# Other places for two hundred operations of the first attention block in a kernel whose order is written out by hand

## The chip, the cores and the metric

The kernel runs on one core of a Trainium2 chip. The metric is device time in microseconds (us) for one execution; a figure for a kernel is the median of its runs. The kernel before was run three times: 416.27, 416.80 and 418.25 us, median 416.8 us.

## What is computed

The input is x of 2048 rows by 512 columns in bf16. Four residual layers follow one another: x + A, x + B, x + A, x + B, each on the layer norm of x.

```python
# A: sliding-window attention, 32 heads of 16, window 256
qkv = layernorm(x) @ wqkv
scores = einsum("bhqd,bhkd->bhqk", q, k) * 16**-0.5      # masked to 0 <= q - k < 256
x = x + (softmax(scores) @ v) @ wo
# B: linear attention, phi(t) = where(t > 0, t + 1, exp(t)) + 1e-6
kv, z = einsum("bhsd,bhse->bhde", phi(k), v), phi(k).sum(s)
x = x + (phi(q) @ kv / (phi(q) @ z)) @ wo
```

## The kernel before, in words

The 2048 rows are cut into four groups of 512 (I = 0 to 3), each of four tiles of 128 rows. For each group of the first layer the kernel makes the layer norm (`ln_tile`), transposes it (`transpose`, into `xnT`), and multiplies by the weights (`proj`): queries into `qT`, keys into `kall` (spread over two columns so that two heads can share a matmul), values into `vst`, from where DMAs scatter them into `vbd`.

The attention itself (`scores`, `pv_group`) goes in runs. One run is 8 to 16 small matmuls on TensorE (L823) that write four banks of PSUM: two banks (the first pair) are read by one exponential on ScalarE (L834), two (the second pair) by another (L837). Both write one of seven `pt` buffers. Then the edges of the window are zeroed in `pt` by masks: on VectorE as a multiplication with a 0/1 tile (`tri`, L852), on GpSimd as `affine_select` (L857), one instruction for each 128x256 piece. When all masks of a set of runs are done, `pv_group` multiplies `pt` by `vbd` on TensorE (L880), and VectorE divides by the sums (L893, L894). The TensorE results of `proj` are taken out of PSUM by VectorE or ScalarE (`evac`, L527, `k_spread`, L786 and L788).

PSUM has eight banks. `psb` is all eight of them, and each operation that takes a bank is told which one. A bank is written again only when its last reader is done, and the wait for that is put in by the framework.

The order of everything is written out in the string `ORDER`. Each word is one operation: its number, the engine that issues it (P TensorE, A ScalarE, V VectorE, G GpSimd, S the SP queue that issues DMAs, H a transfer that has landed, no instruction), and the places that it takes, one digit for each ring. `163P42` is operation 163 on TensorE, a run of scores whose first pair is banks 4 and 5 and whose second pair is banks 2 and 3. `675P5` is the first half of a projection (two matmuls of 512 columns) in bank 5; its second half, `676P`, and the reader of the bank, `677V`, follow. A word such as `2F4` is a fill: two matmuls of the identity into bank 4 whose result nobody reads (L463). Each engine executes its own words strictly in the order in which they stand; how the words of different engines are interleaved has no effect but through the waits for data and for places.

Operations named below: scores 163, 188, 204, 210, 235, 240, 395, 416, 432, 437, 469, 474 with the two exponentials whose numbers follow each (163: 164 and 165; 432: 433 and 434); projections 100/101, 102/103, 358 to 360 (an evacuation, 360, on VectorE), 355 to 357 (keys, 357 on VectorE), 650 to 653 (keys; 653 is the spreading of half of them), 678 to 680 (values), 675 to 677 (queries); masks 213, 409, 420, 421; 422, the first of the `pv_group` operations of group I = 1; 647, the reciprocal root of a layer norm (`rstd`, which takes two instructions on GpSimd, L595 and L596, or two on ScalarE, L592 and L593); 648, 649 and 664, the normalisation that uses it, the DMA transpose of it, and the projection that reads it.

Of the kernel before, what the change touches and what calls it, by code (L numbers as in the profile page):

```python
# [234 lines left out]
494V 495G 493V 507A 693S 943V1 2F4 496P5 179V 501P4 508A 497P 511P06 498P 512A 510V 509G 502P 180V1 499P 47S 503P 513A
500V 504P 181G 516P02 686P5 517A 514V 505V 940S 184V3 518A 3F7 521P06 671P4 45S 48H 687P 522A 519V 947V2 672P 688V 523A
527P20 674V 948S 265P5 266P 529A 524V 526G 661P7 673V 944S 515G 662P 528A 267V 525G 261P6 520V 694P40 663A 689S 531V
532G 262P 695A 530V 533P7 263V 534P 696A 535P 272V0 699P42 538P6 700A 539P 698G 540P 182G01 536P 701A 541P 537V 704P04
273G 705A 542V 952P3 543S1 703G 953P 268V2 706A 709P06 668P2 547S0 954V 669P 710A 274V3 970P3 670V 555S2 711A 715P04
708V 971P 702V 697V 716A 973P7 714G 551S3 972V 974P 707G 712V 717A 731P20 975V 949P6 732A 713V 950P 719G 720V 43S 718V  # L240
733A 951V 2F7 736P42 721P7 722P 738A 723P 734G 726P6 724P 737A 727P 725V 728P 729P 741P24 740G 730V 552P7 739G 743A 553P
977P6 742A 554V 746P40 978P 748A 544P7 979V 545P 747A 744V 752P20 980S 745V 958P6 575V 754A 959P 750G 546V 735G 749V
269G 753A 2F5 768P40 960V 185G 751V 769A 755V 2F7 773P62 756V 757V 8V 774A 186G2 763P5 758P4 764P 567V0 775A 759P 187S
765P 559V1 760P 770A 766P 776G 761P 777G 275S 767V 778P26 270G1 955P0 779A 762V 956P 556P1 780A 957V 976S 783P42 557P
# [1204 lines left out]
```

## Time and profile before

| | |
|---|---|
| runs | 416.27, 416.80, 418.25 us; median 416.8 |
| span of the profiled execution, first to last instruction | 414.3 us |
| TensorE busy | 395.2 us (95%) |
| ScalarE busy | 368.8 us (89%) |
| VectorE busy | 355.0 us (86%) |
| GpSimd busy | 239.2 us (58%) |
| chain that ended last, by engine | PE 66%, ACT 15%, DVE 12%, issue 4%, POOL 2% |

The page gives the span of the profiled execution and no other time of it; the median of the runs is 2.5 us above the span. Times within the trace count from the start of the span. PE is TensorE, ACT ScalarE, DVE VectorE, POOL GpSimd, SPq the SP queue. "L837" is line 837 of the kernel. Where instructions overlap their start and end in an engine's pipeline (two exponentials overlap by a tenth of a microsecond or more), the distance from start to start is what an instruction costs its engine.

### The profile page before, as it was taken

The page shows a single profiled execution, that of the slowest core. Times are in us where ns is not written, and L with a number is a line of the kernel's source. Part 1 is how long each engine was busy: PE and PEld are TensorE (multiplying, and loading weights), DVE is VectorE, ACT ScalarE, POOL GpSimd, SP SyncE. Part 2 cuts the span into 40 slices and gives each one's busy share as a digit, 9 for nine tenths or more (in the row PEclk, how much of TensorE's full clock was granted, in tenths as well). Part 3 has the DMA queues.
Part 4 walks back from the last instruction along what each step waited for, and adds up shares of the span by engine and source line. Part 5 has one row for each costly group of instructions (what it writes and reads, how often), then busy time and mean ns, then how long its engine had stood idle before and what let it go on. Part 6 is the DMA issues. An engine that isn't in the chain of part 4 may idle for free.

```text
span 414.3 us, 15373 instructions
## 1 busy us (share of the span) xinstructions
PE 395.2 (95%) x6277; PEld 219.3 (53%) x6347; DVE 355.0 (86%) x844; ACT 368.8 (89%) x496; POOL 239.2 (58%) x505
## 2 busy tenths in 40 slices
PE   7998999999999999999999999999999999999995
PEld 3565555555555555643565555555555555565342
DVE  5899898888769988689998999998789588889895
ACT  5999999999999999678999999999999999977731
POOL 7578524344576667923774688554427476585432
PEclk9999999999999999999999999999999999999998
DMA  8233226440313122100032212322111311300024
GB/s 245 83 95 100 64 76 110 110 77 24 89 25 80 35 55 26 28 4 0 22 72 41 55 45 64 71 38 53 41 49 34 54 30 40 54 14 14 3 69 138
DMA packets 65306, 24.11 MB, mean 58 GB/s; under 512 B 46160, under 2 KB 65232, under 8 KB 65232
## 3 DMA queue, kind: packets, MB, share of 16 engines
q1 hardware_dynamic: 63168, 21.65, 23.5%
q10 hardware_dynamic: 2064, 1.44, 1.1%
q8 instruction: 50, 0.82, 0.8%
q14 instruction: 24, 0.20, 0.2%
HBM read 6.29 MB, written 2.10 MB: 20 GB/s over the span
## 4 chain that ended last, share of the span: by engine, by line
PE 66%; ACT 15%; DVE 12%; issue 4%; POOL 2%; ACTq 0%; POOLq 0%; DVEq 0%
PE psb L537 41%; PE psb L880 14%; PE psb L823 8%; ACT pt L834 7%; ACT pt L837 7%; DVE pt L852 2%; DVE kall L788 1%; PE psb L995 1%; DVE qT L527 1%; PE psb L566 1%; DVE kall L773 1%; PE psb L463 1%; DVE vst L527 1%; PE psb L1106 1%; DVE ln L661 1%
## 5 line engine op out<-in xcount | busy, mean ns | idle before, releaser
L857 POOL TENSOR_SCALAR_AFFINE_SELECT pt<-pt 128x256 bf16<-128x256 bf16 x285 | 121.3, 453 | 110.2 <-ACT pt L837 66.7
L837 ACT ACTIVATE pt<-psb 128x1024 bf16<-128x1024 f32 (+2 forms) x156 | 156.2, 1017 | 4.4 <-PE psb L823 3.0
L834 ACT ACTIVATE pt<-psb 128x1024 bf16<-128x1024 f32 (+2 forms) x156 | 156.7, 1014 | 3.6 <-PE psb L823 2.3
L880 PEld LDWEIGHTS <-pt 128*128 128x128 bf16 x2880 | 81.4, 96 | 16.5 <-issue 5.0
L880 PE MATMUL psb<-vbd,pt 128*128 128x34 bf16 x2880 | 85.1, 178 | 2.4 <-ACT pt L834 1.0
L537 PE MATMUL psb<-xnT,wA 128*128 128x512 bf16 (+1 forms) x305 | 65.1, 335 | 2.2 <-DVE o_sb L894 0.3
L537 PE MATMUL psb<-wB,xnT 128*128 128x512 bf16 x237 | 62.4, 379 | 1.7 <-issue 0.5
L823 PE MATMUL psb<-qT,kall 32*128 32x256 bf16 (+4 forms) x1664 | 62.6, 242 | 0.6 <-ACT pt L834 0.4
L537 PEld LDWEIGHTS <-xnT 128*128 128x128 bf16 x384 | 33.4, 97 | 37.0 <-issue 5.3
L823 PEld LDWEIGHTS <-kall 32*128 32x128 bf16 x1664 | 28.0, 92 | 45.8 <-issue 42.2
L852 DVE TENSOR_TENSOR pt<-pt,tri 128x512 bf16<-128x512 bf16 (+1 forms) x133 | 49.5, 399 | 2.8 <-ACT pt L837 1.9
L537 PEld LDWEIGHTS <-wA 128*128 128x128 bf16 x320 | 27.4, 97 | 26.1 <-issue 7.7
L537 PE MATMUL psb<-woA,oT 128*128 128x512 bf16 x120 | 32.8, 380 | 1.2 <-issue 0.6
L537 PE MATMUL psb<-wA,xnT 128*128 128x512 bf16 x115 | 32.3, 380 | 1.5 <-ACT pt L837 0.5
L537 PE MATMUL psb<-xnT,wB 128*128 128x512 bf16 x119 | 32.1, 380 | 0.9 <-issue 0.5
L537 PE MATMUL psb<-wkv,pqT 128*128 128x512 bf16 (+1 forms) x126 | 30.2, 373 | 0.5 <-issue 0.2
L894 DVE TENSOR_TENSOR o_sb<-psb,rall 128x256 bf16<-128x256 f32 x64 | 27.2, 424 | 2.4 <-DVE rall L893 0.2
L893 DVE RECIPROCAL rall<-psb 128x16 f32<-128x16 f32 x64 | 16.1, 251 | 13.7 <-PE psb L880 9.4
L661 DVE BATCH_NORM_STATS2 ln<-xres 128x6 f32<-128x512 f32 (+1 forms) x39 | 26.6, 682 | 1.2 <-DMA xres<-in_A_x_dram 1.1
L596 POOL TENSOR_TENSOR ln<-ln,mhalf 128x1 f32<-128x1 f32 x38 | 22.0, 578 | 3.2
L948 ACT ACTIVATE pks<-psb 128x512 bf16<-128x512 f32 x32 | 19.5, 614 | 3.8 <-PE psb L537 3.4
L527 DVE CAST qT<-psb 128x512 bf16<-128x512 f32 (+1 forms) x32 | 19.2, 602 | 3.9 <-PE psb L537 3.7
(133 smaller groups left out, 523.6 us busy)
## 6 DMA issues: line engine op xcount, KB each, us to landing
vbd<-vst SPq DMA_DIRECT2D x128, 34.0 KB, 1.9
wB<-in_B_wqkv_dram SPq DMA_DIRECT2D x6, 256.0 KB, 3.5
out_dram<-ost SPq DMA_DIRECT2D x10, 128.0 KB, 1.8
xres<-in_A_x_dram SPq DMA_DIRECT2D x4, 256.0 KB, 3.2
xnT<-xn SPq DMA_TRANSPOSE x50, 2.4
out_dram<-ost ACTq DMA_DIRECT2D x5, 128.0 KB, 2.8
wA<-in_A_wqkv_dram SPq DMA_DIRECT2D x1, 512.0 KB, 7.5
xres<-in_A_x_dram SPq DMA_DIRECT2D x1, 512.0 KB, 8.7
```

Source lines behind the costliest of these rows:

```text
L527: (nc.scalar.copy if e == "ACT" else nc.vector.tensor_copy)(dst(), src())
L537: nc.tensor.matmul(t["t"][:], lhsT=lhs(c), rhs=rhs(c), start=(c == 0), stop=(c == NCT - 1))
L596: nc.gpsimd.tensor_tensor(out, out, mhalf[:, 0:1], op=ALU.pow)
L661: nc.vector.bn_stats(t["st"], x())
L823: nc.tensor.matmul(psb[:, sT.k + x if x < 2 else sS.k + x - 2, at * 64:(at + w) * 64], lhsT=kbd[half(m)][32 * x:32 * x + 32, tt, m % 4, :, :],
L834: nc.scalar.activation(body[:, 0:2, 0:w_all, :], psb[:, sT.k:sT.k + 2, 0:w_all * 64].rearrange("p x (s c) -> p x s c", c=64), ACT.Exp, sca ...
L837: nc.scalar.activation(body[:, 2:4, 0:w_all, :], psb[:, sS.k:sS.k + 2, 0:w_all * 64].rearrange("p x (s c) -> p x s c", c=64), ACT.Exp, sca ...
L852: nc.vector.tensor_tensor(v, v, mt, op=ALU.mult)
L857: nc.gpsimd.affine_select(out=v, in_=v, compare_op=ALU.is_ge, fill=0.0, base=1 if kind == 0 else -2, pattern=[[0, 4], [2 * sg, 64]], chann ...
L880: nc.tensor.matmul(t["O"][:, x, g, :, :], lhsT=parts[b][0][:, s0:s0 + 2, :], rhs=vbd[half(m)][:, m % 4, :, 4 * tt + g, :], start=(n == 0), ...
L894: nc.vector.tensor_tensor(o_sb[:, u0:u0 + nu, P * tt:P * tt + P].rearrange("p u (h e) -> p u h e", e=DH), Ov[:, :, :, 0:DH], r.to_broadcas ...
L948: nc.scalar.activation(dst(), ps()[:], ACT.Exp)
```

## The change

Only `ORDER` changes. The first words of each engine are the same, and from about 70 us of the trace on each engine has the words that it had, in the order that it had. Between them, from about 20 us on, some two hundred words stand at other places of their engines' orders. Forty-eight operations take other places in rings, most of them banks of PSUM. Twenty-five go to another engine: 11 masks from GpSimd to VectorE (162, 196, 203, 208, 213, 233, 239, 243, 409, 440, 472), 11 masks from VectorE to GpSimd (197, 228, 245, 398, 404, 421, 435, 441, 446, 450, 452), the evacuation 103 from VectorE to ScalarE, the root 647 from GpSimd to ScalarE, and the key spreading 653 from ScalarE to VectorE. On SP some twenty words change places: the scatter 119 goes ahead of 115, the loads 31, 29 and 51 go forward, the load 35 and the scatter 685 go back behind 637 and 681, and the transpose 176 stands beside 172. The number of fills stays, and one of them (3F0) goes to bank 1. The stretch in both orders (the words are wrapped anew from there to the end of the string, which makes the whole diff long):

```diff
-136V 25S 112P0 345V3 151A 149G 113P 152A 159P64 118A 337V31 140G 102P2 114V 161A 35S 128P1 346G 129P 103V 130P 131P 160A
-342V1 163P42 153G 132V 26H 165A 115S 347V2 162G 3F0 188P06 164A 634V1 100P2 189A 166G 141P5 154P4 101V 155P 142P 36H
-143P 190A 635G 144P 28H 352V0 193P02 145V 156P 119S 12G 157P 194A 108P6 158V 167P7 168P 191G 169P 195A 109V 170P 199P04
-171V 348P6 200A 353P3 196G 349V 338P7 172S0 354V 343P6 201A 339V 204P02 638V0 379P7 29S 205A 380P 202G 344V 636V32 192G
-206A 381V 2F5 210P04 361P6 639G 637S 642V1 362P 211A 208G 110P7 363V 212A 31S 203G 224P02 30H 198G 640V0 225A 383P5 213G
-111V 384P 197V 382S 226A 643G 229P06 385V 214P4 215P 230A 646V0 216P 32H 358P5 644V3 231A 647G 217P 228V 235P02 641S
-218V 359P 209G 236A 207G 355P7 360V 219P6 645S 237A 933V2 240P04 356P 241A 648V1 220P 239G 357V 221P 649S 232G 222P 233G
-242A 246P02 227V 387P7 234G 386S 247A 223V 388P 238G 245V 389V 248A 395P04 13G 664P6 396A 665P 249V 934G 390S 250P7 667V
...
-255P6 407A 366V 394S 410P02 256P 398V 257P 411A 404V 409G 258P 678P7 259V 412A 679P 416P04 680V 260S3 417A 657P3 414G
-408V 415G 658P 276V 418A 650P2 264S2 660V 432P06 651P 413V 434A 419G 420V 51S 367P5 421V 368P 433A 659V 422P4 423P 369V
-424P 653A 33S 436G 437P06 425P 438A 652V 427P5 428P 426V 429P 439A 430P 442P02 431V 376P4 443A 440G 377P 942G 34H 370P5
-444A 378V 447P06 371P 441V 935V20 448A 682P4 372V 683P 449A 435V 453P02 684V 675P5 454A 676P 446V 451G 685S 452V 450V
-455A 2F4 469P60 677V 445V 471A 457V 2F4 474P24 458V 456V 49S 937V1 475A 464P1 459P0 465P 476A 460P 466P 41S 461P 470A
...
+150P42 27S 112P0 151A 345V3 113P 149G 152A 25S 28H 118A 159P64 100P1 102P3 128P2 129P 130P 131P 337V22 101V 342V0 114V
+119S 115S 31S 29S 51S 52H 32H 30H 26H 161A 160A 346G 132V 347V3 162V 352V1 163P46 165A 164A 103A 153G 140G 166G 634V3
+3F1 188P06 141P5 142P 143P 144P 154P4 155P 156P 189A 190A 157P 193P02 194A 195A 158V 145V 167P7 168P 169P 108P6 170P
+199P04 109V 171V 353P3 348P2 343P6 338P7 354V 349V 339V 197G 191G 635G 344V 638V2 196V 201A 200A 202G 639G 204P42
+379P7 380P 205A 206A 381V 636V01 642V0 640V2 2F5 210P04 361P6 362P 110P7 211A 176S0 172S1 382S 641S 637S 35S 212A
+224P20 225A 226A 383P5 384P 363V 111V 209G 207G 643G 644V1 213V 198G 192G 229P26 385V 646V1 214P4 215P 216P 217P 230A
+235P02 358P5 359P 231A 647A 203V 208V 218V 233V 360V 648V2 645S 649S 219P6 355P7 237A 236A 356P 933V1 234G 13G 12G
+228G 357V 240P24 220P 221P 222P 242A 241A 246P04 387P7 388P 386S 247A 248A 223V 227V 389V 239V 244G 238G 232G 934G
...
+393V 243V 405P04 364P7 406A 407A 255P6 365P 410P02 256P 941V3 366V 411A 412A 257P 258P 678P7 416P40 679P 657P3 658P
+417A 935V20 945V2 259V 415G 414G 403G 398G 413V 680V 408V 660V 409V 432P64 650P2 651P 418A 419G 421G 420V 394S 260S2
+264S3 49S 367P1 368P 652V 369V 653V 659V 434A 433A 422P0 423P 424P 437P46 425P 427P1 428P 429P 430P 438A 439A 442P42
+426V 431V 376P0 377P 444A 443A 682P1 447P62 683P 370P5 371P 378V 435G 684V 440V 449A 448A 453P02 675P4 676P 445V 372V
+441G 677V 454A 455A 2F4 469P60 2F4 474P24 456V 458V 457V 446G 436G 451G 450G 942G 452G 471A 464P1 459P0 465P 460P 466P
+461P 467P 462P 470A 475A 476A 33S 39S 41S 681S 685S 936S 40H 50H 36H 34H 42H 479P62 473V 937V0 477G 463V 468V 472V
```

## Rows read from the trace of the kernel before

**Rows 1.** Stretches: each engine's busy us (instructions), granted clock, DMA share, GB/s
```profile
core 0: us, PE busy (x) PEld busy (x) DVE busy (x) ACT busy (x) POOL busy (x), PEclk, DMA share, GB/s
20.00:70.00 50.00, 47.70 (x888) 28.98 (x895) 44.67 (x108) 49.54 (x58) 28.21 (x69) 1.00 0.42 97
30.00:40.00 10.00, 9.13 (x188) 5.92 (x187) 9.52 (x21) 10.00 (x12) 7.77 (x20) 1.00 0.46 117
70.00:160.00 90.00, 87.15 (x1576) 49.55 (x1589) 75.55 (x184) 87.71 (x103) 52.04 (x118) 1.00 0.29 60
```

**Rows 2.** Timeline of TensorE near 22 us: start, us, engine, line, operation, count
```profile
21.67 0.37 PE L823 MATMUL psb<-qT,kall 32*128 32x64 bf16 x8
```

**Rows 3.** Timeline of ScalarE, 21.4 to 23.2 us
```profile
21.40 0.91 ACT L834 ACTIVATE pt<-psb 128x896 bf16<-128x896 f32 x1
...
22.19 0.50 ACT L837 ACTIVATE pt<-psb 128x384 bf16<-128x384 f32 x1
...
22.56 0.51 ACT L834 ACTIVATE pt<-psb 128x384 bf16<-128x384 f32 x1
...
23.16 1.02 ACT L834 ACTIVATE pt<-psb 128x1024 bf16<-128x1024 f32 x1
```

**Rows 4.** Groups by line and shape, ScalarE, whole span: count | busy us, mean ns
```profile
L527 ACT CAST qT<-psb 128x256 bf16<-128x256 f32 x6 | 2.3, 382 | 1.6 <-PE psb L537 1.6
...
L592 ACT ACTIVATE ln<-ln,eps 128x1 f32<-128x1 f32 x1 | 0.3, 294 | 0.0
L593 ACT ACTIVATE ln<-ln 128x1 f32<-128x1 f32 x1 | 0.2, 203 | 0.0
```

**Rows 5.** Groups by line and shape, VectorE, 20 to 70 us
```profile
L852 DVE TENSOR_TENSOR pt<-pt,tri 128x512 bf16<-128x512 bf16 x11 | 4.8, 447 | 0.3 <-ACT pt L837 0.3
...
L527 DVE CAST qT<-psb 128x512 bf16<-128x512 f32 x6 | 4.1, 688 | 1.4 <-PE psb L537 1.3
...
L852 DVE TENSOR_TENSOR pt<-pt,tri 128x256 bf16<-128x256 bf16 x11 | 3.5, 327 | 0.0
```

**Rows 6.** Timeline of ScalarE, 47.9 to 54 us
```profile
47.86 1.18 ACT L837 ACTIVATE pt<-psb 128x1024 bf16<-128x1024 f32 x1
...
49.00 1.02 ACT L834 ACTIVATE pt<-psb 128x1024 bf16<-128x1024 f32 x1
49.92 1.02 ACT L837 ACTIVATE pt<-psb 128x1024 bf16<-128x1024 f32 x1
...
51.06 1.02 ACT L837 ACTIVATE pt<-psb 128x1024 bf16<-128x1024 f32 x1
...
52.89 0.95 ACT L786 ACTIVATE kall<-psb,eo 128x256 bf16<-128x256 f32 x2
53.67 1.04 ACT L834 ACTIVATE pt<-psb 128x1024 bf16<-128x1024 f32 x1
```

**Rows 7.** Timeline of TensorE, scores near 48.5, 50.5 and 53 us
```profile
48.56 0.40 PE L823 MATMUL psb<-qT,kall 32*128 32x320 bf16 x12
...
50.48 0.40 PE L823 MATMUL psb<-qT,kall 32*128 32x192 bf16 x8
...
53.10 0.40 PE L823 MATMUL psb<-qT,kall 32*128 32x256 bf16 x8
```

**Rows 8.** Timeline of TensorE, 59 to 60.8 us
```profile
58.96 1.04 PE L537 MATMUL psb<-xnT,wA 128*128 128x512 bf16 x4
59.83 0.59 PE L463 MATMUL psb<-identb 128*128 128x512 bf16 x2
60.36 0.40 PE L823 MATMUL psb<-qT,kall 32*128 32x192 bf16 x8
```

**Rows 9.** Timeline of ScalarE, 60.1 to 62.1 us (two exponentials in one row)
```profile
60.13 1.99 ACT L837 ACTIVATE pt<-psb 128x1024 bf16<-128x1024 f32 x2
```

**Rows 10.** Timeline of VectorE, one mask near 51 us
```profile
51.26 0.62 DVE L852 TENSOR_TENSOR pt<-pt,tri 128x512 bf16<-128x512 bf16 x1
```

**Rows 11.** Timeline of GpSimd, the mask beside it, and what it waited for
```profile
51.00 0.61 POOL L857 TENSOR_SCALAR_AFFINE_SELECT pt<-pt 128x256 bf16<-128x256 bf16 x1 [1.07 <-ACT pt L837]
```

**Rows 12.** Waits of the SP queue, 20 to 70 us: total us, times, longest
```profile
SPq L806 <- DVE vst L527: 8.4, 2, 6.3
```

More of the change, by code (lines that the diff above doesn't have):

```diff
@@ L235 @@
[L235 to L244, printed above, removed]
@@ L340 @@
[L340 to L344 removed]
+24S 2G 5G 14H 53V0 4G 15H 0G 11G 58V1 54A 16H 17H 68A1 63V2 6G 3G 59G 55V20 10F0 56P5 1G 60V0 57A 64G 61P1 18H 62V 9G
@@ new lines @@
+771G 789P04 963V 985P6 271S 781G 790A 986P 786G 987V 791A 788G 183S 2F3 805P20 772G 787V 806A 793V 794G 2F7 810P64
+792V 37S 812A 800P3 38H 801P 802P 807A 795P5 803P 796P 811A 804V 797P 798P 571V2 815P02 813G 329P6 816A 808G 799V
+311P7 330P 560G 817A 820P40 331V 312P 821A 561G21 317P6 313V 822A 819V 826P24 809G 562S 318P 827A 548P7 824G 319V 549P
+818G 823V 828A 825G 989P02 550V 814G 990A 831V 829G 2F6 994P46 830V 568G 995A 832P1 833P 834P 991A 835P 837P5 836V
+838P 996A 839P 563V1 840P 842S0 1000P02 320A0 998G 323P7 841V 1001A 324P 564G 854S2 981P6 325V 1002A 1005P04 569G0
@@ new lines @@
+298P61 1078A 288V 293P31 1044V 289V 294P 299P 333V 295A 301P24 1079A 296V 306P52 300V 307P 297V 1080G 1082P60 308A
+302P 334V 1084A 871G 1051P4 866V1 1056P3 1052P 303A 1057P 1083A 1058P 867G 304V 1053P 305V 1059P 1054P 314A3 860G00
+1088P06 1055V 309P2 1090A 1085G 1060V 610P5 1086G 581P42 1089A 310V 1061S0 862V2 1093P26 611P 1095A 315V 863G 622P1
+861S 612V 623P 1094A 1081G 576P70 624V 864G2 582P 1065S1 326A2 1099P20 327V 577P 1100A 316V 628P6 1098V 629P 868V1
+583A 584P33 1101A 630V 869S 585P 1091V 1062P2 586A 874V 1102G 1113P04 865S 587V 589P61 1115A 1087G 588V 1063P 1097G
@@ new lines @@
+1298P 1555V 1556A11 1276S 1551P 1225V 1299A 1281P1 1557G 1283P2 1552V 1282A 1547P7 1278G 1300S 1548P 1284V 1568A2 925V
+1329P02 1549V 1279G 1285P4 1331A 1301P6 919V 1558G 1240V 1302P 1286V 1330A 1287P5 1280S 1303A 1333P20 1288V 1295P4
+1335A 914V 1289P5 1334A 1560V0 1296A 1304S 1342P06 1336G 1293P2 1344A 1290V 1321P3 1561G 1294V 1322P 1343A 1346P46
+1332G 1323V 1291P2 1347A 1309P1 1348A 1569G 1559S 1292V 1313P3 1564A3 926V 1355P46 1314V 1565G 1317P2 1356A 1324S
+1325P0 1310V 1311P3 1357A 1566G 920V 1326P 1570G 1312A 1359P64 1327V 1847P3 1360A 1349G 1318V 1361A 1567S 1368P60
@@ new lines @@
+1590P7 1463V 1619A 1591P 2178V32 1622P40 1464P6 1623A 1592V 1465P 2179G 1466P 1467P 1624A 1880G 1627P24 1468V 2175P7
+1629A 2176P 1626G 1881V 1874S 1593P6 2177V 1628A 1594P 1615G 1633P04 1625V 1882S 1595V 2169P7 1634A 1632G 2170P 1620G
+1631V 1616V 1630G 2172P6 1635A 2171V 1473S1 1649P02 2173P 1621V 1650A 1637V 1636G 1584P4 2174V 1469S2 1638G 1585P
+1651A 1639P7 1586V 1640P 1641P 2182A0 1652G 1654P20 2186V1 1655A 2183G 1644P6 1877V 1645P 1656A 1642P 1653G 1878S
+1646P 2187G 1643V 1647P 1659P24 1648V 1911P1 1657G 1660A 2180G 1389V0 1912P 1661A 2188G 1664P62 1913V 1474P0 2184V
@@ new lines @@
+1723P02 1711V 1471P 1482G 1725A 1718P6 1472V 1719P 1391G21 1724A 1720P 1485V 1728P42 1713P7 1393V2 1730A 1714P 1392S
+1726G 1721P 1715P 1729A 1722V 1716P 1922S 1733P02 1483V0 1734A 2206P5 1717V 2207P 1727V 1735A 1738P06 2208V 2200P4
+1739A 2201P 1736G 1737V 1732G 1923P5 2202V 1740A 1744P02 1924P 1745A 1731V 1743G 1491P71 1925V 1742G 1492P 1746A 1926S
+1927P04 1493V 1897P6 1928A 1898P 1747V 1749G 1741V 1748V 1929A 1477V1 2F7 1932P20 1755P7 1756P 1934A 1899V 1930G
+1750P4 1757P 1900V 1751P 1933A 1931G 1758P 1394G 1752P 1759V 1753P 1937P02 1754V 1768S2 1908P5 1938A 1936V 1909P
@@ new lines @@
+1798P00 1804V 1805V 1810P 2252A 2080P1 2081P 1811A 2255G 2256P26 2082V 1799P 2244G 2258A 1812V 1789G 2076P1 1813V
+2077P 2257A 2253V 2254G 2270P46 2078V 2271A 1790G0 1806P31 1800V 1807P 2091V0 2272A 1814P22 2249G 1791S 2259G 2275P04
+1808V 1815P 2276A 2248G 2260P7 1816V 2083S3 2261P 2277A 2262P 2092G 2263P 2281P02 2264V 2280G 2088P6 2282A 2095V1
+2089P 2265P7 2283A 2090V 2286P04 2266P 2267P 2287A 2284V 2285G 2230P6 2273V 2279G 2268P 2288A 2292P02 2269V 2231P
+2293A 1822P43 2232V 2093G02 1823P 2103V2 2294A 2322P06 2278G 2094S 2084P5 1824V 2323A 2085P 2295G 2274V 1817P42 2086V
@@ new lines @@
+2324A 2233S 2096G 2327P02 2099V0 2296P5 2329A 2297P 2289G 2298P 2104G 2290V 2299P 2328A 1818P 2300V 2291G 2333P26
+2100G 2097V2 1819A 2113P54 2335A 2098S 2114P 1820V 2105G0 1832P1 1821V 1833P 2334A 2115V 2301P7 2325G 1825P6 1834A
+2338P42 1826V 2326V 2302P 2340A 1835V 2303P 1836V 1842P6 2339A 2304P 2336V 2344P20 2305V 1843P 2345A 2341G 2331V
+1525P4 2306S0 2337G 2342V 2108P50 1844A 2330G 2109P 2332G 2346A 1845V 1520P7 2310S1 1846V 1521P 2110A 2347V 2358P20
+1522A 1526P 2106S 2111V 2112V 2359A 2348P6 2349P 2101V1 2350P 2360A 2121P50 1523V 2102S 1524V 2122P 2351P 1527A 2123V
@@ L345 @@
+2567P 2507S 2577V1 2573G2 2553P1 2582S 2554P 2568V3 2578S 2558P3 2555A 2574A 2559P 2556G2 2545P7 2569A 2560V0 2546P
+2549P0 2561S 2547V0 2557S 2550P 2548A 2551V3 2552S
 """
```

188 lines of the change are left out of this document (81 added, 107 removed).

## The prediction

> **What bounds the kernel now.** I began with the stretches, since the change lies between 20 and 70 us of the trace and the shares of the whole span say nothing about that part. In these 50 us ScalarE is busy 49.54 us, TensorE 47.70, VectorE 44.67 and GpSimd 28.21, at a granted clock of 1.00 [rows 1]. The reader is to see that ScalarE has half a microsecond to spare and that it sets the pace: it runs one exponential after the other, each about 0.92 us after the one before (49.00 to 49.92, [rows 6]). TensorE must write the scores before each of them, and needs the banks that the exponentials before have emptied. So I took the timelines of ScalarE and TensorE next, and looked for the places where an exponential starts later than 0.92 us behind its predecessor: that is where something else is late. In the new order I then asked of each moved word which last reader of its bank, or which engine's queue, it now stands behind. What reaches ScalarE late in this stretch is lost; what is only late on another engine is not.
>
> **The change part by part.** All times are set against the profiled execution, span 414.3 us; the median of the runs, 416.8, is 2.5 us more, and I carry the difference over unchanged.
>
> 1. *The start.* Scores 163 move from banks 4, 5 and 2, 3 to banks 4, 5 and 6, 7. The second pair is now the one that the L834 exponential reads until 21.40 + 0.91 = 22.31 [rows 3]. Scores 163 began at 21.67 [rows 2]; they can now begin at 22.31 plus 0.05 for the semaphore (an exponential follows its scores by 0.04: 49.00 after 48.56 + 0.40, [rows 6, 7]), 0.69 later. Their exponential at 22.19 had waited 0.15 behind their end at 22.04, of which 0.04 is the semaphore, so 0.12 of it is cover: it comes 0.57 late. Then ScalarE also gets the evacuation 103, 0.38 us [rows 4], less 0.10 of overlap (50.02 against 49.92, [rows 6]): 0.28. The next exponential, at 23.16, came 0.19 later than 22.56 + 0.51 - 0.10, which is taken up. Sum: 0.57 + 0.28 - 0.19 = **+0.66**. Bounds: 0.28 (the evacuation alone) and 0.85 (no wait to take up).
>
> 2. *The root 647 on ScalarE* costs 0.29 + 0.20 [rows 4] less 0.10 of overlap: **+0.40**, bounds 0.30 and 0.50.
>
> 3. *Masks.* To VectorE go, before evacuation 360 (the reader of a bank that scores 240 now need), four two-piece masks and two one-piece ones: 4 x 0.447 + 2 x 0.327 = 2.44 us; from it go 103 (0.4, by its cost on ScalarE, [rows 4]), 197 (0.447) and 228 (0.327), 1.17 [rows 5]. VectorE gets 1.27 us more in a stretch where it is busy 9.52 of 10 us [rows 1]. That makes 360 and the keys 357 late by about as much as items 1 and 2 make ScalarE late (1.06), so I cost it at **0**; the cover is this lateness itself, and if it is thinner VectorE's excess comes through (the third rival). Bounds: -0.2 and +1.27. The masks that go to GpSimd lengthen an engine with 22 us free [rows 1]; the last of them, 421, stands behind 415, 414, 403, 398 and 419, and what waits for it is 422 with all the matmuls queued behind it. I find half a microsecond to spare there; without it 422 is late one for one.
>
> 4. *Scores 416 ahead of 679.* The exponential at 49.00 came 0.22 later than 47.86 + 0.92, because scores 416 stood behind both halves of a projection [rows 6, 7]. One half (0.44: four matmuls end to end take 1.04 and two 0.59, [rows 8], so 0.22 for each one more) now follows them. The wait of 0.22 goes. The next one, 51.06 against 49.92 + 0.92, is as long, but scores 432 now take the pair that the exponential just before them reads; I count 0.05 of it. Sum: **-0.27**, bounds -0.44 and 0.
>
> 5. *The key spreading 653 leaves ScalarE*, where it cost 53.67 - 52.89 = 0.78 [rows 6]. But what follows needs scores 437, and 650 has moved from before scores 432 to behind them. From 432 to 437 TensorE took 53.10 - 50.48 = 2.62 us [rows 7]; now 2.62 + 0.44 = 3.06. ScalarE is out of work before 437 comes: the relief turns into a wait, and 437 sets the time. Late so far: 0.66 + 0.40 - 0.27 = 0.79; the exponential behind 437 had 0.13 of cover (53.67 against 53.50 + 0.04), so it comes 0.79 + 0.44 - 0.13 = 1.10 late, of which some 0.1 more is taken up because matmuls that had waited no longer do. **+0.20** for this item; bounds -0.78 (the relief is kept) and +0.44.
>
> 6. *The fill behind a reader.* Projection 675 moves from bank 5 to bank 4, and the fill 2F4 that follows writes bank 4. It filled a wait at 59.83, right behind the projection; now it must itself wait for evacuation 677. The four matmuls begun at 58.96 end at 60.00 [rows 8]; 0.04 and the evacuation of 0.69 [rows 5] make 60.73, 0.05 more the start of the fill, 2 x 0.22 its length: scores 469 begin at 61.22 and not at 60.36, 0.86 late. Their exponential was the second of the pair at 60.13, started at 60.13 + 1.99 - 1.07 = 61.05 [rows 9] and, with the scores done at 60.36 + 0.40, had 61.05 - 60.76 - 0.04 = 0.25 of cover. **+0.61**; bounds 0 (the fill waits for nothing) and 0.86. The fill 2F5 stands behind exponential 205 in the same way, but the scores behind it need the same bank: cost 0, bound 0.44.
>
> 7. *SP.* Of the scatters, loads and transposes that change places none is read within 3 us of its landing, except the transpose 649, which projection 664 needs: its source 648 is some 0.4 us late and 664 itself 1.1 us. Cost 0; 0.4 if that cover goes. Gone is the hold of 6.3 us by the scatter 685, which stood ahead of three weight loads [rows 12]; nothing waited for these.
>
> Sum: 0.66 + 0.40 + 0 - 0.27 + 0.20 + 0.61 = 1.60. Behind 70 us every engine has its old words, and all of them start late by about this; nothing there runs on a clock of its own. So 414.3 + 1.6 = 415.9 in the span and 416.8 + 1.6 = **418.4 us**. With the bounds, not all at once: 417.2 to 419.6.
>
> A rule on the masks: a VectorE mask of two pieces took 0.62 us beside a GpSimd mask that took 0.61, against a mean of 0.447 for its kind [rows 5, 10, 11]. The Trainium skill ("SBUF — State Buffer", section "SBUF: two separate sides") says that a VectorE operation with two SBUF inputs and a GpSimd operation that reads SBUF take one port pair in turn, so that moving masks from one to the other gives no relief. By that rule each pair that meets adds about 0.17 to VectorE; the two rows agree with it. It is the third rival below that it speaks for.
>
> **The rivals.**
> - *Absorbed.* The 1.6 us are given back later. Between 70 and 160 us ScalarE is idle 2.3 us and TensorE 2.9 [rows 1]; if those waits are for something that did not move, they close. Time 416.8 to 417.2. Against it: the waits there are of the three engines on each other, and all three are late.
> - *Faster.* ScalarE keeps the 0.78 of item 5 and both waits of item 4 (-0.44), the fill costs nothing, VectorE gains 0.2: with items 1 and 2 at their low ends (0.58) that is 416.8 - 0.84, some 416.0; only with more waits closing behind it, as many as ScalarE's whole idle half microsecond [rows 1] and another 0.9, is it below 414.7. For it: ScalarE is the pace, and its work shrinks slightly (0.28 + 0.40 - 0.78). Against: TensorE's order makes it wait.
> - *VectorE's excess.* The masks of item 3 meet GpSimd's and take 0.62, not 0.447: four times 0.17 is 0.7, and what exceeds the cover of 1.06 (1.27 + 0.7 - 1.06 = 0.9) falls on scores 240 and keys 357, and from there on ScalarE. It decides as soon as 360 ends later than exponential 237. Time 418.4 + 0.9 = 419.3, and to 420.4 when the masks before 422 do the same.
>
> **How the numbers follow.** A measurement of this kernel tells about 0.5% (2.1 us) from no change: below 414.7 is faster, above 418.9 slower. My forecast has 0.50 (0.36 of it within, 0.14 above), absorbed 0.20 (0.18 within, 0.02 below), faster 0.10 (0.05 and 0.05), VectorE's excess 0.20 (0.01 within, 0.19 above). Together: faster 0.07, within 0.60, slower 0.33. The range 415.6 to 420.4 leaves out about 0.1 on each side.
>
> **What would show it.** In the trace after: scores at about 22.36 in place of 21.67; two short ScalarE instructions of L592 and L593 near 37 us; ScalarE idle for some 0.8 us before the exponential near 54.8; TensorE idle between a projection near 61 us and a fill, and an exponential near 62.7 that waited for scores. Rows at 70 us and beyond the same as before, shifted by 1.6. It is wrong if the exponential that stood at 53.67 comes before 54.2 (the relief is kept), if the fill starts with no wait, if the shift at 70 us is not that at the end, or if VectorE and not ScalarE is what scores 240 wait for.

## The result, and the profile after

The changed kernel takes 421.3 us (median of 6 runs, 419.7 to 422.4), the kernel before beside it 417.2 (6 runs, 416.3 to 418.5): 1.0095 times as long, interval 1.0072 to 1.0118, some 4 us more. I had forecast 418.4 and a range up to 420.4. The profiled execution of the changed kernel took 422.4 us, its span is 420.5. Lines of the changed kernel's own page have numbers that are 3 higher than those of the kernel before (L840 for L837); in the experiments the numbers are those of before.

To see where the time goes I set each operation's rows in the two traces against each other. The table says how much later an exponential ends than in the kernel before, in us, in the order of the trace (148 lies ahead of every edit; 396 follows scores 395, 401 scores 400, 433 scores 432, 438 scores 437, 454 scores 453; 512 ends at 74 us in the kernel before and at 78 in the changed one):

```
exponential            148   165   211   248   396   401   433   438   454   512
near, us of before      19    22    31    41    42    44    52    54    60    74
changed kernel         0.0   0.5   1.0   1.4   2.7   3.3   3.1   3.5   3.7   4.2
forecast                 -   0.6   0.7   1.1   1.1   1.1   0.8   1.0   1.0   1.6
```

So the loss is made where I looked for it, ahead of 70 us, and it stays at 4.24 up to 118 us. (This execution has 2 us more of small steps behind 118 us. The first, 1.08 us at projection 329, is missing in the traces of experiments 1, 2 and 3 and there in others with the same words around it, so I count it to the executions and not to the change.) But 1.9 us of it, between the exponentials 248 and 401, are at a place where I had counted nothing; that is most of the 2.6 us by which the trace exceeds my sum.

The chain of waits shows that place (start, us, what). In the kernel before, the chain leaves VectorE at 37.9 us for ScalarE, which has it until 40.8, and TensorE behind that:

```profile
37.28 0.61 DVE ln L661
37.89 1.06 ACT pt L834
...
39.68 1.12 ACT pt L834
```

In the changed kernel it stays with VectorE to 41.8 us:

```profile
37.97 0.60 DVE qT L530
...
38.66 1.09 DVE xn L675
...
39.77 0.70 DVE ln L664
...
40.68 1.12 DVE kall L776
41.80 0.04 issue
41.84 0.59 PE psb L540
...
42.65 1.06 PE psb L540 x2
```

Read it from below. Projection 387 (41.84) waited for the keys 357 (L776), which read the bank that it needs; the keys stood behind a statistics (933, L664) and a normalisation (648, L675), and the normalisation took 1.09 us. In the kernel before it took 0.38. Here is VectorE in the changed kernel:

```profile
37.55 0.42 DVE L855 TENSOR_TENSOR pt<-pt,tri 128x512 bf16<-128x512 bf16 x1
37.89 0.68 DVE L530 CAST qT<-psb 128x512 bf16<-128x512 f32 x1
38.66 1.08 DVE L675 TENSOR_SCALAR xn<-xres,ln 128x512 bf16<-128x512 bf16 x1
```

and here the same normalisation in the kernel before:

```profile
38.01 0.38 DVE L672 TENSOR_SCALAR xn<-xres,ln 128x512 bf16<-128x512 bf16 x1
```

What lies beside it in the changed kernel is GpSimd at work on the two memsets 13 and 12 (`vbd`), which end at 39.59, 0.15 us before the normalisation does:

```profile
37.64 1.95 POOL L522 MEMSET vbd<- 128x1088 f32 x2
```

In the old order one memset ran at 25.08 and the other at 41.09, neither beside a normalisation. The change put both into GpSimd's idle time ahead of mask 228. I had searched that queue for masks and had not asked what a memset does to its neighbour. The trace of the kernel before could have told me. At 7.87 us, ahead of every edit, a normalisation of the same size runs beside a memset and takes 1.03 us; it too ends 0.15 us after the memset:

```profile
7.87 1.03 DVE L652 TENSOR_SCALAR xn<-xres,lnm,lrs 128x512 bf16<-128x512 bf16 x1
```

```profile
7.75 1.00 POOL L519 MEMSET vbd<- 128x1088 f32 x1
```

The second half of the loss follows from the wait. TensorE in the changed kernel (start, us, engine, line, operation, count, idle before):

```profile
41.84 0.59 PE L540 MATMUL psb<-wA,xnT 128*128 128x512 bf16 x1 [1.04 <-DVE kall L776]
42.65 1.06 PE L540 MATMUL psb<-wA,xnT 128*128 128x512 bf16 x2 [0.22 <-issue]
43.64 0.61 PE L826 MATMUL psb<-qT,kall 32*128 32x192 bf16 x8
44.27 1.51 PE L540 MATMUL psb<-xnT,wA 128*128 128x512 bf16 x4
```

Four matmuls of 512 columns take 1.51 us where they took 1.04 [rows 8], eight small ones 0.61 for 0.40 [rows 7]. The stretches say why (the column behind POOL is the granted clock):

```profile
40.00:41.80 1.80, 0.80 (x17) 0.43 (x14) 1.77 (x4) 1.80 (x3) 0.47 (x3) 1.00 0.21 54
...
43.00:44.00 1.00, 1.00 (x10) 0.14 (x8) 0.26 (x1) 0.10 (x1) 0.83 (x4) 0.50 0.58 131
44.00:45.00 1.00, 0.99 (x6) 0.29 (x3) 1.00 (x3) 0.71 (x1) 0.68 (x2) 0.50 0.16 39
45.00:46.00 1.00, 1.00 (x19) 0.63 (x18) 0.33 (x2) 1.00 (x2) 0.00 (x0) 0.85 0.27 65
46.00:47.00 1.00, 1.00 (x37) 0.76 (x34) 1.00 (x2) 0.49 (x2) 0.00 (x0) 1.00 0.20 51
```

After the wait of 1.04 us TensorE runs at the lower of its two levels, 0.50 (1.2 GHz), until between 45 and 46 us, and at the higher one (2.4 GHz) from 46 us on. In the kernel before it is 1.00 from 20 to 70 us [rows 1].

The other rows that answer to those of before. ScalarE at the start, and the root on it [rows 3, 4]:

```profile
22.74 0.49 ACT L840 ACTIVATE pt<-psb 128x384 bf16<-128x384 f32 x1 [0.43 <-PE psb L826]
...
23.50 0.38 ACT L530 CAST qT<-psb 128x256 bf16<-128x256 f32 x1
...
37.05 0.34 ACT L595 ACTIVATE ln<-ln,eps 128x1 f32<-128x1 f32 x1
37.41 0.20 ACT L596 ACTIVATE ln<-ln 128x1 f32<-128x1 f32 x1
...
57.18 1.02 ACT L837 ACTIVATE pt<-psb 128x1024 bf16<-128x1024 f32 x1 [1.11 <-PE psb L826]
...
65.42 1.02 ACT L840 ACTIVATE pt<-psb 128x1024 bf16<-128x1024 f32 x1 [0.54 <-PE psb L826]
```

TensorE where scores 163 run [rows 2], and at the fill [rows 8]:

```profile
22.28 0.34 PE L826 MATMUL psb<-qT,kall 32*128 32x64 bf16 x8
...
62.55 1.04 PE L540 MATMUL psb<-xnT,wA 128*128 128x512 bf16 x4
64.37 0.59 PE L466 MATMUL psb<-identb 128*128 128x512 bf16 x2 [0.78 <-DVE qT L530]
64.89 0.40 PE L826 MATMUL psb<-qT,kall 32*128 32x192 bf16 x8
```

### The profile page after: what moved, and what is told of

It is laid out like the page before. It is cut to its first block, busy times and chain, and to the rows that moved or that the text cites. A ratio compares the mean times of both kernels' runs of the same rounds, so it can differ in the third digit from the quotient of the medians.

```text
span 420.5 us, 15369 instructions
## 1 busy us (share of the span) xinstructions
PE 397.4 (94%) x6278; PEld 219.3 (52%) x6347; DVE 357.0 (85%) x844; ACT 369.2 (88%) x497; POOL 237.5 (56%) x502
## 4 chain that ended last, share of the span: by engine, by line
PE 63%; ACT 14%; DVE 11%; issue 5%; POOL 4%; DMA 2%; SPq 0%; ACTq 0%; DVEq 0%; POOLq 0%
PE psb L540 38%; PE psb L883 13%; PE psb L826 8%; ACT pt L840 6%; ACT pt L837 6%; DVE pt L855 2%; DVE qT L530 1%; DVE kall L776 1%; DMA oT<-o_sb 1%; DVE ln L664 1%; PE psb L569 1%; PE psb L998 1%; DVE vst L530 1%; DVE kall L791 1%; PE psb L1109 1%
## 5 line engine op out<-in xcount | busy, mean ns | idle before, releaser
L837 ACT ACTIVATE pt<-psb 128x1024 bf16<-128x1024 f32 (+2 forms) x156 | 155.3, 1009 | 7.3 <-PE psb L826 6.1
L840 ACT ACTIVATE pt<-psb 128x1024 bf16<-128x1024 f32 (+2 forms) x156 | 155.6, 1012 | 6.5 <-PE psb L826 4.5
L540 PE MATMUL psb<-xnT,wA 128*128 128x512 bf16 (+1 forms) x307 | 66.0, 337 | 2.5 <-DMA xnT<-xn 0.5
L855 DVE TENSOR_TENSOR pt<-pt,tri 128x512 bf16<-128x512 bf16 (+1 forms) x133 | 51.1, 409 | 4.8 <-ACT pt L840 2.3
L664 DVE BATCH_NORM_STATS2 ln<-xres 128x6 f32<-128x512 f32 (+1 forms) x39 | 26.6, 682 | 1.6 <-DMA xres<-in_A_x_dram 1.5
L599 POOL TENSOR_TENSOR ln<-ln,mhalf 128x1 f32<-128x1 f32 x37 | 21.4, 579 | 3.1
L957 DVE SCALAR_TENSOR_TENSOR pks<-psb,pks 128x512 bf16<-128x512 f32 x32 | 21.8, 685 | 0.6
```

Source lines behind the costliest of these rows:

```text
L540: nc.tensor.matmul(t["t"][:], lhsT=lhs(c), rhs=rhs(c), start=(c == 0), stop=(c == NCT - 1))
L599: nc.gpsimd.tensor_tensor(out, out, mhalf[:, 0:1], op=ALU.pow)
L664: nc.vector.bn_stats(t["st"], x())
L837: nc.scalar.activation(body[:, 0:2, 0:w_all, :], psb[:, sT.k:sT.k + 2, 0:w_all * 64].rearrange("p x (s c) -> p x s c", c=64), ACT.Exp, sca ...
L840: nc.scalar.activation(body[:, 2:4, 0:w_all, :], psb[:, sS.k:sS.k + 2, 0:w_all * 64].rearrange("p x (s c) -> p x s c", c=64), ACT.Exp, sca ...
L855: nc.vector.tensor_tensor(v, v, mt, op=ALU.mult)
```

## The experiments

All measure one question: which word of the new order costs what. "Later" is again against the kernel before, by the same exponentials as above:

```
exponential                              148   211   248   396   401   433   454   512   run, us
changed kernel                           0.0   1.0   1.4   2.7   3.3   3.1   3.7   4.2   421.3
 + fill in the wait                      0.0   0.9   1.3   1.8   2.0   1.7   2.4   2.9   420.0
 + 933 ahead of 648                      0.0   0.9   1.3   1.3   1.3   1.1   1.7   2.3   419.1
 + fill in another bank                  0.0   1.0   1.4   2.6   3.3   3.1   3.7   3.6   420.0
 + 933 ahead of 648, and
     3 masks to GpSimd                   0.0   0.9   1.3   1.3   1.3   1.1   1.7   2.3   420.1
     root 647 on GpSimd                  0.2   1.1   1.5   1.5   2.7   2.5   3.1   3.6   420.0
     650 ahead of 432                    0.0   0.9   1.3   1.3   1.8   1.9   2.2   2.7   420.2
     load 35 behind 649                  0.1   0.9   1.3   1.3   1.3   1.1   1.7   2.3   419.7
     mask 162 on GpSimd                  0.1   0.9   1.3   1.3   2.1   1.9   2.5   3.0   419.7
     load 35, mask 162, fill             1.1   1.9   2.3   2.3   2.3   2.1   2.7   2.6   418.0
kernel before
 + masks on other engines                1.3   1.5   2.0   2.0   2.0   2.0   2.0   2.1   417.8
 + memsets moved                         1.2   1.0   1.0   1.0   1.1   1.1   1.1   1.1   416.8
 + SP's order                            0.4   0.3   3.6   3.6   3.6   3.6   3.6   3.6   421.1
```

Where the first column is not 0, the execution was late before any edit, and that much is to be taken off the columns behind it. Two executions of one kernel can be 2.7 us apart (the changed kernel, 419.7 to 422.4), so single medians tell no steps of a few tenths; for these I go by the traces.

**1. Does the clock cost, or the wait?** Four filling matmuls go into the wait:

```diff
-246P04 387P7 388P
+246P04 4F3 387P7 388P
```

> The changed kernel with four filling matmuls into the free bank 3 directly ahead of projection 387, so that TensorE works through the 1.04 us in which it waits for the keys 357. Nothing else moves. Theory A (the wait lets TensorE's granted clock fall to 0.73 and 0.68 in 40 to 46 us, and the slower matmuls cost 1.3 us more than the wait itself): the clock stays at 1.00 there, projection 387 still starts near 41.8, but the matmuls behind it are back to 0.38 each and the exponential after scores 400 comes 1.2 to 1.4 us earlier than in the changed kernel's trace; time 1.0 to 1.4 us less than the changed kernel's 421.3, so 419.9 to 420.3. Rival B (the slow stretch is set by something else that is late there, a transpose or a scatter, and the clock only follows): the fills run, the scores and exponentials keep their times within 0.2 us, 421.3. Rival C (the clock falls whatever fills the wait): clock near 0.7 again, 421.3.

Measured: 420.0 us, 1.0083 times before (1.0059 to 1.0106). TensorE of this kernel, and its stretch of 41.5 to 44 us:

```profile
41.20 1.02 PE L463 MATMUL psb<-identb 128*128 128x512 bf16 x4 [0.52 <-ACT pt L834]
42.06 1.03 PE L537 MATMUL psb<-wA,xnT 128*128 128x512 bf16 x4
43.02 0.40 PE L823 MATMUL psb<-qT,kall 32*128 32x192 bf16 x8
43.34 1.04 PE L537 MATMUL psb<-xnT,wA 128*128 128x512 bf16 x4
```

```profile
41.50:44.00 2.50, 2.50 (x19) 0.92 (x18) 1.98 (x7) 2.03 (x3) 2.33 (x7) 1.00 0.35 81
```

The clock stays at 1.00, projection 387 starts 0.2 us *later* (the fill is in its way), and yet the exponential after scores 400 comes 1.33 us earlier than in the changed kernel; 0.13 of that was there at 31 us already, ahead of the edit. So the low clock costs 1.2 us at least (the fill itself makes the projection 0.2 us later), and theory A stands.

**2. Is it the memset that makes 648 long?** Two VectorE words swap:

```diff
-360V 648V2 645S 649S 219P6 355P7 237A 236A 356P 933V1 234G
+360V 933V0 648V2 645S 649S 219P6 355P7 237A 236A 356P 234G
```

> The changed kernel with two VectorE operations swapped: the statistics 933 now come ahead of the normalisation 648, so that 648 no longer runs beside the second of the two GpSimd memsets (37.64 to 39.59 in the trace). Theory A (648 took 1.08 us instead of some 0.4 because of the memset beside it, and what it lost went on to the keys 357 and to projection 387): 648 takes 0.38 to 0.42, keys 357 end 0.6 to 0.7 earlier, TensorE's wait ahead of 387 shrinks from 1.04 to about 0.4; time 0.6 us less (420.7), and up to 2.0 less (419.3) if the shorter wait no longer lets the clock fall. Rival B (648 is long because its own inputs or its tile are late): it stays at 1 us, and so does the time, 421.3. Rival C (the statistics are slowed by the memset as well): 933 grows from 0.87 to 1.5, and the time stays at 421.3.

Measured: 419.1 us, 1.0065 (1.0042 to 1.0087). VectorE of this kernel, whose memsets run from 37.51 to 39.46:

```profile
38.36 0.68 DVE L661 BATCH_NORM_STATS2 ln<-xres 128x6 f32<-128x512 bf16 x1
39.17 0.43 DVE L672 TENSOR_SCALAR xn<-xres,ln 128x512 bf16<-128x512 bf16 x1
39.52 1.21 DVE L773 TENSOR_TENSOR kall<-psb,eo 128x1024 bf16<-128x1024 f32 x1
```

The statistics run beside the memsets at their usual 0.68 us; the normalisation comes when they are nearly over and takes 0.43. The keys are 1.06 us earlier than in the changed kernel, projection 387 follows the scores ahead of it within 0.11 us, the clock stays at 1.00, and 1.95 us of the 4.24 are gone: the upper end of what theory A gave. Over all fourteen traces, those of the experiments below included: in six, 648 begins with most or all of a memset still to run, takes 0.97 to 1.25 us and ends 0.13 to 0.15 us after the memset; in seven it has no memset beside it or one that is nearly over, and takes 0.38 to 0.44; in one it takes 0.57 beside masks of GpSimd, and ends 0.15 us after one of them. In experiments 1 and 3 it begins 0.15 us before the first memset ends and gets through only behind the second. No run leaves 648 ahead of 933 and takes the memsets away; that the memset makes it long, and not the order, rests on this count and on experiment 4, where the memsets alone move and 648 goes from 0.38 to 0.97 us.

The Trainium skill ("SBUF — State Buffer", section "Who interferes with whom") says that `tensor_scalar` can enter a mode in which VectorE needs the port pair that it shares with GpSimd, and that the one that comes second is blocked until the first is done. The traces agree: the normalisation (TENSOR_SCALAR) ends with the memset and not before. The same section says that a two-input operation is not disturbed by a GpSimd operation that only writes; the mask at 37.55 reaches 0.33 us into the memset and takes 0.42, as a mask alone does.

**3. The fill behind a reader.** One digit, in the first of the two fills behind 677:

```diff
-441G 677V 454A 455A 2F4 469P60 2F4 474P24
+441G 677V 454A 455A 2F7 469P60 2F4 474P24
```

> The changed kernel with one digit changed: the first two-matmul fill after projection 675 goes to bank 7, which is free, and no longer to bank 4, which evacuation 677 still reads. Theory A (the sixth item of the prediction: the fill waits for the evacuation, 0.78 us of idle TensorE, and scores 469 with it): the idle time goes, scores 469 start 0.85 to 0.95 us earlier against projection 675 than in the changed kernel, and 0.55 to 0.85 of it is left at 80 us; time 420.5 to 420.7. Rival B (VectorE or ScalarE holds the same place at once, as the exponential behind it waits for its predecessor): less than 0.2 us is left at 80 us, 421.2.

Measured: 420.0 us, 1.0075 (1.0055 to 1.0096); in the trace 0.62 us earlier than the changed kernel behind the fill, and level with it (0.02) ahead of it. The fill now follows the projection at once:

```profile
62.54 1.04 PE L537 MATMUL psb<-xnT,wA 128*128 128x512 bf16 x4
63.41 0.59 PE L463 MATMUL psb<-identb 128*128 128x512 bf16 x2
63.94 0.45 PE L823 MATMUL psb<-qT,kall 32*128 32x192 bf16 x8
```

The sixth item of the prediction, 0.61, is shown, its size too.

**4. The memsets alone, in the kernel before.**

```diff
-236A 207G 355P7 360V
+236A 207G 12G 13G 355P7 360V
```

(and both words taken from their old places)

> The kernel before with nothing but its two GpSimd memsets 12 and 13 moved into GpSimd's idle time behind mask 207, where the second one comes to lie beside the normalisation 648; the masks behind them come 0.8 us later, with nothing waiting for them within 3 us. Theory A (a VectorE normalisation beside a memset waits for it, and keys 357 to projection 387 have only 0.06 us of slack in the kernel before): 648 takes 0.9 to 1.1 instead of 0.38 us, projection 387 starts 0.5 to 0.7 later, and the kernel before becomes 0.5 to 0.7 us slower, or up to 2.0 slower if TensorE's clock falls after the wait: 417.7 to 419.2 against 417.2. Rival B (VectorE's lateness is covered there, as the prediction had it, since ScalarE is the pace): 648 may be longer, the time stays within 0.2 us of 417.2.

Measured: 416.8 us, 0.9999 (0.9984 to 1.0015): theory A's mechanism is there, and its price is not.

```profile
39.04 0.97 DVE L672 TENSOR_SCALAR xn<-xres,ln 128x512 bf16<-128x512 bf16 x1
```

648 takes 0.97 us and projection 387 starts 0.53 us later than the exponentials around it, but the next exponential is not late at all. In the kernel before the projection has half a microsecond of cover, that is, it can come that much later before anything waits for it. TensorE waits 0.68 us here, and its clock stays at 1.00. In the changed kernel projection 387 is 2.21 us behind its time in the kernel before, 0.81 more than the exponential 248, and TensorE waits 1.04 us: there the cover is passed, and the clock falls. Which words make the 0.28 us between the two cases no run shows alone; the changed kernel differs by VectorE's additional masks and by having 648 ahead of the statistics 933, which the kernel before has behind them.

**5. Masks back to GpSimd.** On top of experiment 2:

```diff
-213V 198G 192G 229P26 ... 203V 208V 218V ... 234G 13G 12G 228G
+198G 192G 213G 203G 208G 13G 12G 229P26 ... 218V ... 234G 228G
```

> The changed kernel with statistics 933 ahead of normalisation 648 (as in the run that had 419.07 us), and with three masks, 203, 208 and 213 (1.0 us of VectorE), given back to GpSimd, ahead of its two memsets, so that these end before 648. Theory A (with 648 out of the memsets' way VectorE's 1.27 us of additional masks are covered, as the prediction's third item had it: the keys 357 are 1.15 us late there and the exponentials 1.27): keys 357 end 0.9 to 1.0 earlier, the exponentials keep their times within 0.15 us, 419.0. Rival B (VectorE sets the pace from 28 to 42 us): the exponential after scores 395 comes 0.5 to 1.0 us earlier and this stays to the end: 418.1 to 418.6.

Measured: 420.1 us, 1.0076 (1.0051 to 1.0100), and in the trace 0.03 us at 512. The keys 357 gain 0.15 and no more, since VectorE, no longer busy without a break, waits for the other engines (0.22 us for an exponential ahead of one mask). 648 takes 0.40. Theory A is right in what counts, wrong in that the keys would be a full microsecond earlier: with 648 out of the memsets' way these three masks of the third item cost nothing, as the prediction had it. The cover is the one that it named: in experiment 2 the keys end 1.15 us later than in the kernel before, the exponential 248 1.27.

**6. The masks alone, in the kernel before.** The eight that stand ahead of the keys 357 change engines:

```diff
-162G ... 196G ... 203G ... 208G ... 213G ... 233G ... 197V ... 228V
+162V ... 196V ... 203V ... 208V ... 213V ... 233V ... 197G ... 228G
```

> The kernel before with the engines of eight masks of the changed kernel alone: 162, 196, 203, 208, 213 and 233 go from GpSimd to VectorE (2.2 to 2.4 us), 197 and 228 the other way (0.77); every other operation keeps its place and engine. VectorE has some 1.5 us more before the keys 357, and ScalarE is not late here. Theory A (projection 387 follows the keys by 0.06 us, and behind it are some 0.5 us of cover up to the exponential, as the run with the memsets alone showed): keys 357 1.3 to 1.6 late, exponentials 0.8 to 1.1 late at 44 us, with an idle TensorE of about 1 us ahead of 387 the clock may fall and cost 1.3 more; time 0.8 to 2.4 us above the kernel before, 417.7 to 419.3. Rival B (ScalarE is the pace and VectorE catches up in its own waits): within 0.3 us of the kernel before, 416.9.

Measured: 417.8 us, 1.0021 (1.0008 to 1.0034); 2.05 - 1.28 = 0.77 us in the trace, 0.24 of it at 31 us and 0.5 at exponential 241. So the masks do have a price where the start and the root bring no lateness. But the 0.5 is not the excess that the third item named ("if it is thinner VectorE's excess comes through"): projection 387 follows its scores within 0.08 us, and the clock stays at 1.00. The chain of waits takes another road, through GpSimd:

```profile
36.84 0.29 POOL ln L595
...
38.01 1.30 POOL pt L857 x3
...
39.35 0.24 PE psb L880 x3
39.60 0.39 PE psb L823 x16
```

VectorE, with its additional masks, has the statistics of a layer norm late; the root 647, which is on GpSimd in this kernel, waits 2.13 us for them; three masks stand behind the root, and `pv_group` on TensorE waits for these. The changed kernel has the root on ScalarE and not this road, so the 0.5 is no price of the third item in it.

**7. The root, the half projection, the load, mask 162.** Each on top of experiment 2:

```diff
-646V1 ... 231A 647A 203V
+646V1 647G ... 231A 203V
```

> The changed kernel with 933 ahead of 648 (419.07 us), and the root 647 back on GpSimd ahead of mask 234, the second item of the prediction undone alone. Prediction's step: ScalarE is the pace and 0.40 us leave it: exponentials 0.4 earlier from 37 us on and to the end, 418.7. Rival (VectorE, 1.15 us late at the keys 357, is the next bound): the exponentials are 0.4 earlier at 38 to 42 us, but from the exponential after scores 395 on only 0.1: 419.0.

```diff
-432P64 650P2 651P
+650P2 432P64 651P
```

> The changed kernel with 933 ahead of 648 (419.07 us), and the half projection 650 back ahead of scores 432, the fifth item of the prediction undone in its cause. Prediction's step (scores 437 come 0.44 late since 650 stands ahead of them and behind 432): the exponential behind 437 comes 0.2 to 0.4 us earlier, 418.7. Theory A (TensorE works without a gap from 46 to 62 us, so that 437 comes at the same time whichever of 650 and 432 is first, and items 4 and 5 were two sides of one thing: exponentials that ran ahead and were caught up): exponentials 434 and 433 0.1 to 0.4 later, the one behind 437 unchanged within 0.1, 419.07.

```diff
-637S 35S 212A ... 645S 649S
+637S 212A ... 645S 649S 35S
```

> The changed kernel with 933 ahead of 648 (419.07 us), and on SP the load of weights 35 moved from ahead of the transposes 645 and 649 to behind them. In that run projection 664 started at 42.49, 0.29 us after the scores ahead of it had ended, 3.2 us after its source 648. Theory A (the load holds up the transposes, and with VectorE out of the way 664 waits for them; the cover that the prediction's seventh item named is gone): 664 follows the scores without a gap, the exponential after scores 400 comes 0.25 to 0.35 us earlier, and this stays: 418.8. Rival B (664 waits for the transposes' own flight of some 3 us, whatever is ahead of them): 664 and the exponentials keep their times within 0.1, 419.07.

```diff
-347V3 162V 352V1 ... 166G
+347V3 352V1 ... 166G 162G
```

> The changed kernel with 933 ahead of 648 (419.07 us), and mask 162 back on GpSimd behind mask 166, where GpSimd is idle. Theory A (the first item cost 0.88 to 1.01 us at 31 us instead of 0.66 since mask 162 makes the evacuations 158 and 145 on VectorE 0.55 late, and the second half of scores 199 waits for 145's bank): scores 199 run in one piece of 0.40, the exponential after them comes 0.15 to 0.3 us earlier, of which 0.1 to 0.25 is left at 80 us. Rival B (TensorE's own order is what makes 199 late): no difference at 31 us.

(The 42.49 in the third of these counts from the first instruction that does work; in the profile it is 42.79.)

Measured: 420.0 us, 1.0058 (1.0037 to 1.0080), for the root; 420.2, 1.0076 (1.0054 to 1.0098), for the half projection; 419.7, 1.0066 (1.0044 to 1.0088), for the load; 419.7, 1.0055 (1.0031 to 1.0080), for mask 162. Three of the four traces are spoilt at the same place, projection 664, which now waits for the transposes. Here it is with mask 162 moved, and with the half projection moved:

```profile
43.55 1.02 PE L537 MATMUL psb<-xnT,wA 128*128 128x512 bf16 x4 [1.01 <-DMA xnT<-xn]
```

```profile
43.25 1.02 PE L537 MATMUL psb<-xnT,wA 128*128 128x512 bf16 x4 [0.75 <-DMA xnT<-xn]
```

With the root moved the wait is longest:

```profile
44.14 1.02 PE L537 MATMUL psb<-xnT,wA 128*128 128x512 bf16 x4 [1.28 <-DVE pt L852]
```

(The profile puts this wait, and those of experiments 2 and 5, down to a mask of VectorE that 664 does not read; in experiment 2 that mask had ended 0.9 us before.) The four matmuls take 1.02 us behind each of these waits: the clock is at 1.00 after 1.01 and 1.28 us of waiting, where it was at 0.50 after 1.04 in the changed kernel. The wait is 0.29 in experiment 2 and 0.26 in experiment 5, and none where the load 35 goes behind the transposes: there, and where it goes with other repairs (8 below), 664 follows its scores at once. That speaks for the load as what holds the transposes up; how long differs between executions. In experiment 2 itself the 0.29 cost nothing: with it gone the exponential 401 gains 0.08, not the 0.3 that theory A gave.

What can still be read from the other three: the root leaves ScalarE and exponential 237 comes 0.4 us earlier against its neighbours, but the root delays the memsets on GpSimd, 648 is beside them again (0.98 us), and the run says nothing on the end. With 650 ahead of 432, the exponentials 433 and 438 are at 1.93 and 2.00, against 1.80 at 401: measured from 401, 433 is 0.36 later than in experiment 2, and 438 the same. That is theory A: from 46 to 62 us TensorE hardly pauses (busy 15.74 of 16 us in the changed kernel), and which of two operations is first changes who waits, not when both are done. Mask 162 makes scores 199 one piece of 0.40, and the exponential behind them gains 0.05: rival B.

**8. Repairs together, and SP's order alone.** The first puts experiments 2, 3, the load and mask 162 together; the second gives the kernel before SP's new order and nothing else:

```diff
-24 95 91 27 25 35 115 119 172 29 637 31 382 641 645 649 386 390 176 ...
+24 95 91 27 25 119 115 31 29 51 176 172 382 641 637 35 645 649 386 ...
```

> The changed kernel with four repairs at once: 933 ahead of 648, the load 35 behind the transposes, mask 162 back on GpSimd, and the fill after projection 675 in bank 7. Theory A: the gains add up in part, 1.96 + 0.3 + 0.15 + 0.62 = 3.0 of the 4.24 us at 80 us; what is left, some 1.2, is the start (scores 163 behind the exponential of bank pair 6, 7) and the root 647 on ScalarE: 417.9 to 418.4 and not below the kernel before. Rival B (each repair only exposes the next wait, on VectorE or the transposes): 2.0 to 2.4 us are gained and not more, 419.

> The kernel before with nothing but SP's new order of loads, scatters and transposes. Prediction's seventh item: nothing is read within 3 us of its landing but transpose 649, so 0, and 0.4 us if that cover goes: 416.9 to 417.3. Theory A: the same place decides, projection 664 starts 0 to 0.5 later behind its scores and everything else keeps its time: 416.9 to 417.4. Rival B (the hold of 6.3 us by scatter 685 that the old order has did cost something, and the new order gives it back): 0.3 to 0.8 us below the kernel before, 416.1 to 416.6.

Measured: 418.0 us, 1.0022 (1.0005 to 1.0038), for the repairs: in the trace 2.63 - 1.10 = 1.53 us are left of 4.24, as theory A had it roughly, and the kernel before is still the faster. SP's order alone: 421.1 us, 1.0109 (1.0076 to 1.0143), which no theory had. VectorE waits 2.65 us, in a place where the changed kernel has none: normalisation 644 writes the buffer of 636 again, and transpose 637 must have read it before; TensorE then waits 1.95 us, and its clock is low behind that:

```profile
38.13 0.41 DVE L672 TENSOR_SCALAR xn<-xres,ln 128x512 bf16<-128x512 bf16 x1 [2.65 <-DMA xnT<-xn]
```

```profile
37.50:40.00 2.50, 0.37 (x5) 0.17 (x4) 1.84 (x5) 0.81 (x1) 1.62 (x5) 0.97 0.48 127
40.00:42.00 2.00, 1.77 (x29) 1.03 (x29) 1.97 (x4) 1.17 (x2) 2.00 (x4) 0.50 0.48 47
```

In the new order SP issues transpose 641 ahead of 637, and that fits the buffers that the change gives the normalisations (there it is 648 that writes the buffer of 640 again), not the old ones. So this run does not price the seventh item; it shows that the two orders belong together.

## Why the prediction was wrong

The sum was 1.60, the trace has 4.24 at 80 us. By its steps, each from exponential to exponential of the table:

- *Item 1, the start: 0.66 forecast, 1.01 measured.* Scores 163 came at 22.28 (forecast 22.36), their exponential 0.55 late (0.57), the evacuation took 0.38. What I missed is behind it: TensorE, late by 0.6, then waits 0.41 us for an exponential and scores 199 come late. Of the excess, 0.13 is in this execution and in that of experiment 3 alone (the others have 0.88 or less). Mask 162 on VectorE was a suspect and is at most 0.05 of it; the rest is only read from the trace.
- *Item 2, the root: 0.40, measured 0.39,* in two instructions near 37 us as forecast.
- *Item 3, costed at 0: this is the step that failed,* with 1.91 us between exponentials 248 and 401 and 0.07 right behind. What the step reckoned with was right as far as it went: with 648 out of the memset's way the keys are no later than the exponentials, by the cover that the step named, and three masks given back change nothing (experiment 5). But the step asked only how much work each engine gets, not what runs beside what, nor what a wait does to TensorE's clock. The normalisation beside the memset took 0.7 us more; projection 387 fell 0.81 us further behind than the exponential 248; TensorE waited 1.04 us; its clock fell. The measured price is above the step's own upper bound of 1.27. The swap of experiment 2 takes 1.95 us away, 0.13 of which was there before it; of the 1.8 at least 1.2 are the clock's by experiment 1, and at most 0.6 the wait's.
- *Items 4 and 5: -0.27 and +0.20 forecast, -0.30 and +0.60 measured* (0.43 of the +0.60 up to exponential 438, the rest up to 454). Their mechanisms are in the rows (a wait of 1.11 us ahead of the exponential at 57.18, where I gave some 0.8), but I had priced them one by one on ScalarE. TensorE has hardly a gap from 46 to 62 us, so what 416 gained had to be given back; I took an advance for a gain.
- *Item 6, the fill: 0.61 forecast, 0.56 measured* at 80 us, 0.62 by experiment 3.
- *Item 7, SP: 0.* In the changed kernel true; the cover of 664 that it named is the next to go when the keys come earlier.

Of the rivals, VectorE's excess was nearest: its time, 419.3 to 420.4, its engine and its rule (VectorE and GpSimd in each other's way). Its place was wrong. Its condition, 360 ending later than exponential 237, was met by 0.04 us, and the masks meeting GpSimd's masks are not what cost. Absorbed and Faster fell.

The sentence that misled closes the first part of the prediction: that only what reaches ScalarE late is lost. I took it from the busy shares of the whole stretch. The chain of waits has ScalarE from 37.9 to 40.8 us in the kernel before and VectorE and TensorE around that; in the new order VectorE has it from 34 to 42 us and TensorE from there to 63.
